# One load of V in two transfers, in every third batch: a grouped-query attention backward kernel on one core

## The chip, the cores and the metric

The kernel runs on one core of one Trainium2 chip. The metric is the device time of one execution in microseconds (us); the time of before is the median of three runs. The core has a matrix engine (PE), a vector engine (DVE), a scalar engine (ACT), a general engine (POOL) and a synchronisation engine (SP). Here SP issues the loads and POOL issues the stores; sixteen DMA engines carry both.

## The reference

Grouped-query attention, forward and backward, in bf16: 32 batches, 32 query heads on 4 key/value heads, 4 queries, 2048 keys, depth 128.

```python
def _fwd_reference(q, k, v):            # q [32,32,4,128], k and v [32,4,2048,128]
    k = jnp.repeat(k, rep, axis=1)
    v = jnp.repeat(v, rep, axis=1)
    scale = D ** -0.5
    scores = jnp.einsum("bhqd,bhkd->bhqk", q, k) * scale
    p = _softmax(scores, axis=-1)
    return jnp.einsum("bhqk,bhkd->bhqd", p, v)

def reference(q, k, v, grad_out):
    ...
    _out, _vjp = jax.vjp(_f, q, k, v)
    _grads = _vjp(grad_out)
    return (_out, *_grads)              # out, dq, dk, dv
```

K, V, dK and dV are 2 MB a batch each. So each batch reads 4 MB and writes 4 MB, and everything else is small beside that.

## The kernel before

A batch is one unit of work. Its 128 query rows (8 query heads x 4 queries for each of 4 key/value heads) fill the 128 partitions, and its 2048 keys lie as 128 partitions of 16 keys. Partition p of head h holds keys 16p to 16p+15, which are 4096 bytes in a row in memory.

The steps of a batch b have names, and three strings (HEAD, STEADY, TAIL) write out by hand in which order they are issued; every engine works through its own part of that order. One pass of STEADY is one batch long and mixes steps of several batches:

- LK(b) and LV(b) issue the loads: four transfers for K and four for V, one for each head, each [128 partitions x 4096 bytes], 512 KB, on SP's queue (lines 154 and 160). Both stand in the order one batch and more ahead of their use.
- KT and VT (helper `turned`, line 181) turn K and V on PE with an identity matrix; DVE copies the result out of PSUM (line 183).
- S and EX make the scores and the exponentials (lines 198, 211, 222); NRM makes the normalisers on POOL (line 231); ET and dST turn the rows (line 248).
- O and dQ gather over the keys (line 264), from the V tile and the K tile as loaded. dP makes the score gradients (line 338).
- dV and dK (helper `outer`, line 303) are outer products, eight steps each; ACT copies each from PSUM into an output tile (line 307), and after the eighth POOL issues the tile's two stores of 1 MB (line 326).

K has three buffers, V has two, and dK and dV share four output tiles. A load can be issued when its buffer has been read for the last time, and an output tile can be refilled when its two stores have landed.

Each transfer raises a semaphore sixteen times when its parts land. SP's transfers take eight such semaphores in turn, so that a transfer also waits until the eighth transfer before it on SP has landed. With eight loads a batch, that is the load in the same place one batch earlier. POOL's transfers take eight others.

Of the kernel before, what the change touches and what calls it, by code (L numbers as in the profile page):

```python
# [81 lines left out]
def kernel(ctx: ExitStack, tc: tile.TileContext, q, k, v, grad_out, out_0, out_1, out_2, out_3):  # L82
    nc = tc.nc
    B, Hq, Sq, D = q.shape
    NH, Sk = k.shape[1], k.shape[2]
    P = 128
# [41 lines left out]
    v_v = v.rearrange("b h (p c) d -> b h p (c d)", c=C)  # L128
# [27 lines left out]
    def LV(b):  # L156
        S = st[b]
        S["v"] = v_pool.tile([P, NH, C, D], BF16, name="v_sb")
        for h in range(NH):
            nc.sync.dma_start(out=S["v"][:, h].rearrange("p c d -> p (c d)"), in_=v_v[b, h])  # L160

    def bank16():

# [170 lines left out]
    def dP(b, i):  # L334
# [6 lines left out]
        banks.give(t)  # L341

    table = {"LK": LK, "LV": LV, "QDT": QDT, "O": O, "dQ": dQ, "NRM": NRM}
    for i, c in enumerate("ab"):
        for n, f in (("S", S_), ("EX", EX), ("dP", dP), ("ET", ET), ("dST", dST)):
# [16 lines left out]
    with tc.manual_schedule():  # L362

        for w in HEAD.split():
            w, b = w.split("@")
# [5 lines left out]
        for w in TAIL.split():  # L371
            w, b = w.split("@")
# [31 lines left out]
```

## Time and profile before

| | |
|---|---|
| median of three runs | 701.2 us (699.08, 701.52, 701.2) |
| the profiled execution's own time | 698.71 us |
| its span, first to last instruction | 696.7 us |
| granted clock of PE, mean | 0.980 |
| busy: PE, DVE, ACT, POOL | 626.0, 584.5, 569.1, 302.7 us |
| bytes moved by DMA | 274.44 MB, mean 394 GB/s |
| loads on SP's queue (q1, hardware) | 37920 packets, 134.50 MB |
| transfers on POOL's queue (q0, software) | 37536 packets, 138.16 MB |
| instruction fetches (q8) | 96 packets, 1.57 MB |

A packet is what one DMA engine moves at one time: here a row of 4096 bytes in most cases. The trace keeps the start, the duration, the size and the queue of every packet, and the time of each of the sixteen landings of every transfer. It does not keep which of the sixteen engines a packet or a landing belongs to.

The profile's busy shares are averages over the span. The span has a start of some 40 us in which the first loads come in, a long stretch in which one pass of STEADY follows another, and an end of some 40 us after the last load.

### The profile page before, as it was taken

The numbers are of one execution on the slowest core, as the hardware profiler recorded it, in microseconds if no ns is written. First come the engines' busy times: TensorE is split into PE (matmuls) and PEld (weight loads), VectorE is DVE, ScalarE is ACT, GpSimd is POOL, SyncE is SP. The second block draws the span as 40 slices with busy tenths as digits, with TensorE's granted clock in tenths as the row PEclk, the third lists the DMA queues.
The fourth block names the chain that finished last, engine by engine and source line by source line (L and its number), as shares of the span: only waits on it lengthen the run. The fifth ranks groups of instructions, "written<-read, shape, count | busy, mean of one in ns | idle before, by whom it ended". The sixth has DMA issues, their size and how long they took to land.

```text
span 696.7 us, 28064 instructions
## 1 busy us (share of the span) xinstructions
PE 626.0 (90%) x12352; PEld 454.1 (65%) x12352; DVE 584.5 (84%) x992; ACT 569.1 (82%) x673; POOL 302.7 (43%) x506
## 2 busy tenths in 40 slices
PE   5899999999998989979999798998998889998982
PEld 4577776677676656666666676667766677666661
DVE  5999999999997998869988688888988869898960
ACT  0698989899887989869888687887888868888994
POOL 1355443555454435443354424544434543345452
PEclk9999999999999999999999899999999989999997
DMA  9989999999999999999999999999999999999767
GB/s 339 400 317 411 417 415 416 416 413 415 417 415 417 414 417 416 417 409 412 415 415 413 373 397 398 400 410 382 416 416 417 415 340 393 415 414 415 289 257 274
DMA packets 75577, 274.44 MB, mean 394 GB/s; under 512 B 8448, under 2 KB 8448, under 8 KB 75456
## 3 DMA queue, kind: packets, MB, share of 16 engines
q0 software_dynamic: 37536, 138.16, 49.3%
q1 hardware_dynamic: 37920, 134.50, 48.9%
q8 instruction: 96, 1.57, 0.8%
q14 instruction: 25, 0.20, 0.1%
HBM read 136.31 MB, written 136.31 MB: 391 GB/s over the span
## 4 chain that ended last, share of the span: by engine, by line
PE 43%; DMA 33%; ACT 6%; DVE 5%; POOL 5%; issue 5%; SPq 0%; POOLq 0%; DVEq 0%; ACTq 0%
PE banks L181 18%; DMA k_sb<-in_k_dram 15%; DMA out_dram<-dk 12%; PE banks L303 10%; PE banks L264 7%; ACT dv L307 5%; PE banks L248 5%; DMA out_dram<-dv 4%; PE banks L198 3%; POOL dop L231 2%; DMA v_sb<-in_v_dram 2%; DVE kt L183 2%; DVE ds L338 1%; ACT dk L307 1%; POOL qp L231 1%
## 5 line engine op out<-in xcount | busy, mean ns | idle before, releaser
L307 ACT CAST dv<-banks 128x1024 bf16<-128x1024 f32 x256 | 245.5, 1028 | 56.9 <-PE banks L303 56.3
L307 ACT CAST dk<-banks 128x1024 bf16<-128x1024 f32 x256 | 250.7, 1025 | 34.5 <-PE banks L303 23.6
L183 DVE COPY kt<-banks 128x1024 bf16<-128x1024 bf16 x256 | 164.3, 680 | 8.3 <-PE banks L181 8.3
L183 DVE COPY vt<-banks 128x1024 bf16<-128x1024 bf16 x256 | 166.2, 680 | 1.3 <-PE banks L181 0.9
L181 PE MATMUL banks<-ident,k_sb 128*128 128x128 bf16 x2048 | 145.8, 221 | 13.1 <-DMA k_sb<-in_k_dram 8.6
L181 PE MATMUL banks<-ident,v_sb 128*128 128x128 bf16 x2048 | 143.5, 220 | 14.3 <-ACT dv L307 9.7
L231 POOL TENSOR_SCALAR dop<-do_sb,rinv 32x128 bf16<-32x128 bf16 x128 | 76.7, 599 | 181.3 <-PE banks L303 118.9
L181 PEld LDWEIGHTS <-k_sb 128*128 128x128 bf16 x2048 | 120.8, 99 | 41.9 <-issue 31.7
L181 PEld LDWEIGHTS <-v_sb 128*128 128x128 bf16 x2048 | 122.2, 98 | 28.7 <-issue 23.3
L303 PE MATMUL banks<-dop,e 64*128 64x256 bf16 x1024 | 99.3, 276 | 15.1 <-POOL dop L231 11.3
L326 POOL DMA_DIRECT2D out_dram<-dv x62 | 43.7, 709 | 138.0 <-ACT dv L307 67.6
L338 DVE SCALAR_TENSOR_TENSOR ds<-banks,delta,e 128x1024 bf16<-128x1024 f32 x64 | 82.2, 1284 | 17.3 <-PE banks L198 14.3
L303 PE MATMUL banks<-qp,ds 64*128 64x256 bf16 x1024 | 86.4, 272 | 2.1 <-ACT dk L307 1.4
L231 POOL TENSOR_SCALAR qp<-q_sb,srinv 32x128 bf16<-32x128 bf16 x128 | 78.1, 610 | 10.7
L222 ACT ACTIVATE e<-banks,negb 128x1024 bf16<-128x1024 f32 x64 | 70.7, 1111 | 8.6 <-DVE negb L214 8.5
L211 DVE TENSOR_REDUCE m<-banks 128x1 f32<-128x1024 f32 x64 | 75.1, 1215 | 0.9 <-PE banks L198 0.9
L303 PEld LDWEIGHTS <-e 64*128 64x128 bf16 x1024 | 34.0, 94 | 63.1 <-issue 46.7
L250 DVE COPY et<-banks 128x1024 bf16<-128x1024 bf16 x64 | 41.3, 686 | 29.6 <-PE banks L248 29.6
L303 PEld LDWEIGHTS <-ds 64*128 64x128 bf16 x1024 | 42.2, 94 | 28.8 <-ACT dv L307 13.1
L326 POOL DMA_DIRECT2D out_dram<-dk x62 | 44.0, 713 | 13.6 <-DMA out_dram<-dk 13.0
L250 DVE COPY dst<-banks 128x1024 bf16<-128x1024 bf16 x64 | 43.5, 681 | 5.5 <-PE banks L248 3.6
L248 PE MATMUL banks<-ident,ds 128*128 128x128 bf16 x512 | 39.4, 221 | 7.1 <-ACT dk L307 6.8
(39 smaller groups left out, 484.1 us busy)
## 6 DMA issues: line engine op xcount, KB each, us to landing
k_sb<-in_k_dram SPq DMA_DIRECT2D x128, 512.0 KB, 13.8
v_sb<-in_v_dram SPq DMA_DIRECT2D x128, 512.0 KB, 18.6
out_dram<-dv POOLq DMA_DIRECT2D x64, 1024.0 KB, 23.6
out_dram<-dk POOLq DMA_DIRECT2D x64, 1024.0 KB, 22.1
out_dram<-o_sb POOLq DMA_DIRECT2D x32, 32.0 KB, 23.2
out_dram<-dq_sb POOLq DMA_DIRECT2D x32, 32.0 KB, 16.2
q_sb<-in_q_dram POOLq DMA_DIRECT2D x7, 128.0 KB, 21.9
do_sb<-in_grad_out_dram POOLq DMA_DIRECT2D x7, 128.0 KB, 22.0
```

The costliest lines, as they stand in the source:

```text
L181: nc.tensor.transpose(out=ps[:, 4 * hh + j, :], in_=S[which][:, 2 * (i % 2) + hh, 4 * (i // 2) + j, :], identity=ident[:])
L183: nc.vector.tensor_copy(out=S[f"{which}t{i}"][:], in_=ps)
L211: nc.vector.reduce_max(out=S["m"][:, i:i + 1], in_=S[f"s{i}"][1], axis=AX.X)
L222: nc.scalar.activation(out=S[f"e{i}"][:], in_=ps, func=ACT.Exp, bias=S["negb"][:], scale=scale, accum_out=S["l"][:, i:i + 1],)
L231: nc.gpsimd.tensor_scalar(out=t[r, h % 2, :], in0=src[r, :], scalar1=by[r, :], scalar2=None, op0=ALU.mult)
L248: nc.tensor.transpose(out=ps[:, u, :], in_=S[f"{src}{i}"][:, P * u:P * u + P], identity=ident[:])
L250: nc.vector.tensor_copy(out=S[f"{name}{i}"][:], in_=ps)
L264: nc.tensor.matmul(ps[G * h:G * h + G, :], lhsT=S[f"{xt}{c // 8}"][:, c % 8, G * h:G * h + G], rhs=S[kv][:, h, c, :], start=(c == 0), stop ...
L303: nc.tensor.matmul(ps[:, a, :, c, :], lhsT=S[f"{x}{i // 4}"][r, u:u + P], rhs=S[y][r, :, :], start=True, stop=True, tile_position=(2 * G * ...
L307: copy(out=S[name][:, :, 2 * i:2 * i + 2, :].rearrange("p h c d -> p h (c d)"), in_=banks.ap(t).rearrange("p a (j w) -> p (a j) w", j=2),)
L326: store.dma_start(out=dst[b][:, 2 * a:2 * a + 2, :], in_=o[:, 2 * a:2 * a + 2].rearrange("p h c d -> p h (c d)"))
L338: nc.vector.scalar_tensor_tensor(out=S[f"ds{i}"][:], in0=ps, scalar=S["delta"][:], in1=S[f"e{i}"][:], op0=ALU.subtract, op1=ALU.mult,)
```

## The change

In LV, the load of the fourth head (h = 3) is issued as two transfers, one of partitions 0 to 118 (119 rows) and one of partitions 119 to 127 (9 rows), in every third batch from batch 3 on: batches 3, 6, 9 and so on to 30, ten in all. All other loads stay as they are, and so do the bytes and the order of the steps.

```diff
@@ -157,7 +157,9 @@
         S = st[b]
         S["v"] = v_pool.tile([P, NH, C, D], BF16, name="v_sb")
         for h in range(NH):
-            nc.sync.dma_start(out=S["v"][:, h].rearrange("p c d -> p (c d)"), in_=v_v[b, h])
+
+            for r in (slice(0, 119), slice(119, P)) if h == NH - 1 and b % 3 == 0 and b else (slice(0, P),):
+                nc.sync.dma_start(out=S["v"][r, h].rearrange("p c d -> p (c d)"), in_=v_v[b, h, r])
```

## The prediction

> **What bounds the kernel now.** I read the page's slices first, then the windows by stage, the chain of waits, SP's own waits, and last the trace's records of packets and landings.
>
> ```profile
> span 696.7 us, 28064 instructions
> PE 626.0 (90%) x12352; PEld 454.1 (65%) x12352; DVE 584.5 (84%) x992; ACT 569.1 (82%) x673; POOL 302.7 (43%) x506
> DMA  9989999999999999999999999999999999999767
> GB/s 339 400 317 411 417 415 416 416 413 415 417 415 417 414 417 416 417 409 412 415 415 413 373 397 398 400 410 382 416 416 417 415 340 393 415 414 415 289 257 274
> ```
>
> No compute engine is full, but the DMA row is full until the last tenth, at 415 to 417 GB/s in slice after slice. The windows by stage (us, busy times, clock, DMA share, GB/s) say the same:
>
> ```profile
> 40.00:120.00 80.00, 78.11 (x1620) 57.17 (x1607) 74.03 (x128) 72.37 (x87) 37.79 (x62) 1.00 1.00 397
> 120.00:240.00 120.00, 113.67 (x2262) 82.35 (x2264) 108.67 (x184) 105.00 (x125) 57.23 (x94) 1.00 1.03 415
> 400.00:560.00 160.00, 147.75 (x2846) 106.37 (x2843) 138.50 (x234) 134.35 (x159) 68.91 (x113) 0.98 1.02 406
> ```
>
> PE is nearly full to 120 us and has gaps from there on. The chain of waits between 195 and 262 us shows what fills them: three times a wait of 17 us for a K load, with 4 us of PE work between.
>
> ```profile
> 199.11 16.95 DMA k_sb<-in_k_dram
> ...
> 220.24 16.81 DMA k_sb<-in_k_dram
> ...
> 241.24 17.01 DMA k_sb<-in_k_dram
> ```
>
> Pass follows pass every 21.1 us there, and 19.5 us between 53.3 and 72.8 us, where PE's L181 leads the chain. So compute needs 19.5 us a batch, and DMA sets 21.1.
>
> Next, is it all sixteen DMA engines, or some? The landing records answer. For the fourth V load of a batch (us from the start; 1st, 7th, 8th, 15th, 16th landing):
>
> | batch | 1st | 7th | 8th | 15th | 16th |
> |---|---|---|---|---|---|
> | 7 | 140.8 | 143.1 | 143.7 | 144.9 | 147.2 |
> | 13 | 264.1 | 265.4 | 267.7 | 268.8 | 274.3 |
> | 17 | 343.7 | 345.1 | 351.6 | 353.2 | 358.6 |
> | 27 | 556.4 | 558.3 | 558.7 | 562.7 | 570.4 |
>
> A load is whole only at its 16th landing. By batch 17 the sixteen have parted into seven early ones, eight later ones, and one alone. That one engine comes last by 5 to 9 us. From batch 7 to 13 the 7th landing moves on by 20.4 us a batch, the 8th and 15th by 20.65, the 16th by 21.18; the 16th holds 21.2 to batch 27. So **one slow DMA engine paces the kernel**, and the other fifteen have slack of 0.5 to 0.8 us a batch. Its packets are long: between 674.05 and 675.20 us it alone still has stores, with packets of 160 to 176 ns (mean 169), where 159 ns is the usual row and the next starts 4 ns before the end (a pitch of 155).
>
> **The change, part by part.** Removed: ten loads of 128 rows. Before, 32768 packets of 4096 bytes make 256 loads, so each load is 16 equal shares of 8 rows. Added: ten of 119 and ten of 9 rows.
>
> *The shares.* No row shows a transfer of 119 rows. The bounds are: shares as even as can be (15 engines with 8 rows or fewer; nothing changes), or equal shares as all 256 loads have them. 119 is 7 x 17, so equal shares on at most sixteen engines mean seven engines with 17 rows; nine rows are nine engines with one. I take the equal shares, because every load of before has them. Then seven engines carry 17 or 18 rows instead of 8, and at least seven of the others carry none. By the Trainium skill ("DMA: Bandwidth & Descriptors", the section on why a DMA increments its semaphore by 16) the engine count is the largest divisor up to 16 and the lowest-numbered engines are taken; that would be 7 and 9, and this split.
>
> *What it costs the seven.* Ten more rows x 155 ns = 1.55 us a changed batch, 0.52 us a batch on average. *What it saves the others:* 7 or 8 rows; on the slow engine at 165 ns (between 159 and 169, both queues mixed) 1.16 to 1.32 us, 0.39 to 0.44 a batch.
>
> *The sum, if the seven are the early seven.* The slow engine goes from 21.18 to 20.76, the seven from 20.4 to 20.9 (from packets alone, 128 x 0.155 + 0.4 for small ones = 20.25, to 20.8). The new pace is 20.8 to 20.9, still above compute's 19.5. The DMA-paced stretch runs from batch 3's V (whole at 58.7 us) to batch 31's (655.8 us): 28 batches x 0.28 to 0.38 = 8 to 10.6 us. I take 9.5. On the profiled 698.7 us that is 689.2; that execution lay 2.5 us under the median of 701.2, so I state 691.5 as the median.
>
> *Issue and waits on SP.* Ten more issues of 0.33 us (the row of L160) are 3.3 us on a queue that is idle for most of a batch: nothing. But the eight semaphores shift by one. SP already waits there:
>
> ```profile
> SPq L154 <- PE banks L303: 293.5, 29, 13.4
> SPq L160 <- PE banks L303: 80.2, 27, 5.1
> SPq L160 <- DMA v_sb<-in_v_dram: 72.3, 46, 2.5
> ```
>
> The nine rows wait for the first K load of the same batch, which lands 1.9 to 2.8 us after the fourth V load's issue from batch 7 to 27. Each V load of the next batch waits for its right-hand neighbour, 2.5 us later. Queued behind on SP are only later loads. What covers it is the slow engine's backlog: loads take 21 us from issue to landing, so 2.6 us off that queue starve nobody. Without cover it is 10 x 2.6 = 26 us.
>
> *Nine rows as a transfer of their own.* Back-to-back loads at the start land 1.27 us apart (6.36, 7.63, 8.96), which is 8 x 0.155 plus a semaphore packet of 9 ns; I see no fixed price. The same page's rules for kernel authors advise against two transfers to disjoint partitions, and its fixed part is about 2.0 us each: by that, 10 x 2.0 = 20 us slower if none of it overlapped. The start of this trace disagrees with such a price between queued transfers.
>
> *Landing of the split load.* On the seven, ten rows interleaved with stores are up to 3.1 us. The 15th landing leads the 16th by 5 to 9 us from batch 13 on, so it stays hidden; at batches 3, 6 and 9 the lead is 0.7 to 3.1 us, but SP's semaphore isn't yet the limit there. Nothing added.
>
> **The rivals.**
> *B, slower: the slow engine is one of the seven.* It then gets ten more rows x 0.165 = 1.65 us, ten times: 16.5 us on an engine with no slack, 717.7. It decides as soon as the slow one is among the seven. For it: counted blindly, 7 in 16. Against: the groups of 7, 8 and 1 look like halves of eight, one half with the odd one in it; I put an odd one at an end of a half, and seven counted from one end of the sixteen then take it in one place of four. That is my choice, no row shows it. By the same skill page ("Latency and other measured facts") engines 7 and 15 are usually the slow ones, which the lowest seven would spare; this trace has one slow engine, not two.
> *C, nothing: the slow one is spared, but the seven lie in the later eight.* These go from 20.65 to 21.17, as slow as the slow engine was: 701, within 4 us. For it: the eight are more than the seven. What sets them back are the 96 instruction fetches of 16 KB (the one followed at 427 us cost 1.15 us with the row behind it): 110 us over eight engines and 32 batches is 0.43 us a batch, about their distance.
> *N: 119 rows are spread nearly evenly.* 701. Against: the equal shares so far.
> *L: the waits on SP's shifted semaphores show.* 5 to 26 us slower, 706 to 727. For it: V comes just in time (weight loads wait for it 21 times, 0.7 us at the longest). Against: the backlog.
>
> **How the numbers follow.** My forecast, A, has 0.44; C 0.27; B 0.19; L 0.06; N 0.04. A measurement of this kernel can tell about 0.5% (3.5 us) from no change. A is faster but for 0.01; C splits 0.05 faster, 0.12 same, 0.10 slower, since seven engines near the bound seldom wait less than one. So faster 0.43 + 0.05 = 0.48; same 0.12 + 0.04 = 0.16; slower 0.01 + 0.10 + 0.19 + 0.06 = 0.36. A alone lies in 687 to 697. The range runs from 686 (a relief of 1.32 us fully kept is 13 us, and two more) to 712, which takes in C, N and the lower part of L; it leaves out B, the rest of L and A's edge, 0.2 or a little more.
>
> **What would show it.** In the landings of a 119-row load, nine of sixteen would come at once, seven late. The 16th landing of the fourth V load should move on by about 20.85 us a batch, and the lone engine's distance should shrink. The waits of 17 us for K should shorten. Landings parted further, with passes near 21.7 us, would mean B; an unchanged pace with a smaller lone distance C; no early landings N; longer SP waits at L160 with idle DMA slices L.

## The result and the profile after

The changed kernel takes 721.1 us (median; 720.52 to 721.87) beside 700.77 us for the kernel before on the same chip: a ratio of 1.0298, 95% interval 1.0277 to 1.0319. It is slower by 20 us. The forecast A (691.5 us, faster) is wrong, and so is the range to 712 us; the rival B stood at 717.7 us.

The page of the changed kernel (its profiled span, then the DMA row in 40 slices, GB/s in the same slices, and the shares of the chain of waits):

```profile
span 718.9 us, 28084 instructions
...
DMA  9989999999999999999999999999999999999667
GB/s 334 384 323 412 416 415 416 398 415 414 384 389 395 415 393 362 412 393 393 369 391 391 379 400 402 372 379 409 400 410 389 396 380 358 383 416 412 259 238 277
...
DMA 48%; PE 38%; DVE 4%; ACT 4%; issue 4%; POOL 1%; SPq 0%; POOLq 0%; ACTq 0%; DVEq 0%
```

The bytes are the same and the DMA row still shows nines, but from the eighth slice on the rate falls below 400 GB/s again and again, where it lay at 409 to 417 from slice 4 to slice 22 before. The nines hide it: they are means over sixteen engines, in tenths. Of the chain, DMA holds 48%. In the kernel before it held 33%:

```profile
PE 43%; DMA 33%; ACT 6%; DVE 5%; POOL 5%; issue 5%; SPq 0%; POOLq 0%; DVEq 0%; ACTq 0%
```

The windows by stage have the same loss, in 120 to 240 us for instance (us, busy PE, PEld, DVE, ACT, POOL, clock, DMA share, GB/s), 401 GB/s for 415:

```profile
120.00:240.00 120.00, 107.58 (x2177) 77.72 (x2164) 100.66 (x172) 97.94 (x116) 55.73 (x92) 0.99 1.02 401
400.00:560.00 160.00, 142.46 (x2844) 104.67 (x2848) 134.55 (x229) 128.56 (x154) 64.60 (x107) 0.99 1.01 393
```

The chain of waits from 228 to 300 us shows where the time goes. Batch 12 is a split one, its fourth V load is issued at 242.29 us, and the K load behind it is the second line:

```profile
230.69 16.64 DMA k_sb<-in_k_dram
...
251.54 20.83 DMA k_sb<-in_k_dram
...
276.55 17.01 DMA k_sb<-in_k_dram
```

The wait for K behind a split V load is 20.8 us, the others are 17 us as before: about 4 us in one pass. The landing records say which part of the transfer is late (us from the start, landings in order). The first record of each line comes 0.4 to 0.5 us after the issue, ahead of all queued loads, and I read it as carrying no data. The prediction expected nine early landings of the 119 rows in its place; the trace has this one.

```
batch 12, 119 rows, issued 242.29: 242.7 | 252.1 252.5 256.1 256.7 257.6 257.9 | 266.9
batch 12,   9 rows, issued 245.01: 245.5 | 248.8 249.5 252.5 252.9 256.5 257.2 258.0 258.3 | 267.4
batch 21, 119 rows, issued 441.73: 442.2 | 450.2 450.3 451.0 451.0 451.4 452.7 | 464.6
```

119 rows land in seven shares and 9 rows in nine, as the equal shares had it. But one of the seven, and one of the nine, lands 9 to 12 us after all others: the lone engine is in both. Over the ten split loads this distance of the 119 rows grows from 0.3 us in batch 3 and 3.2 us in batch 6 to 11 to 14 us from batch 15 on. On that engine the load before, of 8 rows, lands at 261.49, the 17 rows at 266.90 and the one row at 267.36. So 18 rows take 5.9 us where the 8 rows before took 2.7 (from 258.75).

### The profile page after: what moved, and what is told of

The parts are those of the page before. It is cut to its first block, busy times and chain, and to the rows that moved or that the text cites. A ratio compares the mean times of both kernels' runs of the same rounds, so it can differ in the third digit from the quotient of the medians.

```text
span 718.9 us, 28084 instructions
## 1 busy us (share of the span) xinstructions
PE 629.3 (88%) x12352; PEld 458.2 (64%) x12352; DVE 588.0 (82%) x992; ACT 568.9 (79%) x673; POOL 301.7 (42%) x506
## 4 chain that ended last, share of the span: by engine, by line
DMA 48%; PE 38%; DVE 4%; ACT 4%; issue 4%; POOL 1%; SPq 0%; POOLq 0%; ACTq 0%; DVEq 0%
DMA k_sb<-in_k_dram 48%; PE banks L183 17%; PE banks L305 10%; PE banks L266 6%; PE banks L250 3%; ACT dv L309 3%; PE banks L200 2%; DVE kt L185 1%; DVE m L213 1%; DVE ds L340 1%; ACT dk L309 1%; DVE vt L185 1%; POOL dop L233 0%; PE banks L173 0%; POOL out_dram L321 0%
## 5 line engine op out<-in xcount | busy, mean ns | idle before, releaser
L185 DVE COPY kt<-banks 128x1024 bf16<-128x1024 bf16 x256 | 166.3, 683 | 22.2 <-PE banks L183 21.9
L183 PE MATMUL banks<-ident,k_sb 128*128 128x128 bf16 x2048 | 151.9, 225 | 31.0 <-DMA k_sb<-in_k_dram 26.6
L183 PE MATMUL banks<-ident,v_sb 128*128 128x128 bf16 x2048 | 145.9, 221 | 24.3 <-ACT dv L309 10.7
L183 PEld LDWEIGHTS <-k_sb 128*128 128x128 bf16 x2048 | 124.0, 101 | 62.0 <-issue 31.2
L183 PEld LDWEIGHTS <-v_sb 128*128 128x128 bf16 x2048 | 123.7, 99 | 39.2 <-issue 21.8
L305 PE MATMUL banks<-dop,e 64*128 64x256 bf16 x1024 | 97.2, 273 | 10.8 <-issue 6.0
L233 POOL TENSOR_SCALAR qp<-q_sb,srinv 32x128 bf16<-32x128 bf16 x128 | 77.3, 604 | 10.7
L200 PE MATMUL banks<-vt,qdt 128*32 128x512 bf16 x512 | 40.6, 385 | 3.1 <-ACT dv L309 1.5
```

Of the source, the lines that this page charges most:

```text
L183: nc.tensor.transpose(out=ps[:, 4 * hh + j, :], in_=S[which][:, 2 * (i % 2) + hh, 4 * (i // 2) + j, :], identity=ident[:])
L185: nc.vector.tensor_copy(out=S[f"{which}t{i}"][:], in_=ps)
L200: nc.tensor.matmul(ps[G * h:G * h + G, a, :], lhsT=S["qdt"][:, col, G * h:G * h + G], rhs=xt[:, 4 * (h % 2):4 * (h % 2) + 4, :].rearrange( ...
L233: nc.gpsimd.tensor_scalar(out=t[r, h % 2, :], in0=src[r, :], scalar1=by[r, :], scalar2=None, op0=ALU.mult)
L305: nc.tensor.matmul(ps[:, a, :, c, :], lhsT=S[f"{x}{i // 4}"][r, u:u + P], rhs=S[y][r, :, :], start=True, stop=True, tile_position=(2 * G * ...
```

## The experiments

All are the changed kernel with another rule for which rows of V make one transfer. Only the tuple in the loop header differs, so the diffs show that line. Unless said otherwise they change V's fourth head in batches 3, 6, ... 30.

**Which engine is the slow one.** Single parts of r and 16 - r rows, with r from 1 to 8, are probes: r equal shares of one row take the first r engines, if every transfer takes them in the same order.

```diff
- (slice(0, 119), slice(119, P)) if h == NH - 1 and b % 3 == 0 and b else ...
+ (slice(0, 112), slice(112, 105 + b // 2 + 4), slice(105 + b // 2 + 4, P)) if h == NH - 1 and b % 2 == 0 and 8 <= b <= 22 else ...
```

> Batches 8, 10, ... 22 load V's fourth head as 112 + r + (16 - r) rows, with r = 1, 2, ... 8. Theory S (one slow DMA engine, and it is one of the seven that took the 119 rows): the part of r rows has r landings, one row each, and from some r on, between 1 and 7, its last landing comes late by the lone engine's distance (4 to 9 us after the others); all parts of 16 - r rows (9 to 15 landings) have that late landing too. Theory T (the late landing of the 119 rows belonged to the transfer, as its last share, and not to an engine): the parts of r rows have no late landing at any r from 1 to 8. Time under S: within 4 us of before, since each engine gets 7, 8 or 9 rows.

The one run of it took 698.43 us. Landings with data of the parts of r rows:

```
r=3  244.8 245.2 246.1
r=4  284.7 284.7 286.1 286.5              (112 rows of the same load: 282.5 ... 290.5, 297.2)
r=5  327.0 327.3 327.4 327.7 | 340.1      (112 rows: 326.6 ... 333.2, 339.6)
r=6  368.4 368.5 368.9 369.2 372.4 | 383.1
r=8  455.5 455.5 455.6 455.6 455.7 457.2 457.4 | 469.5
```

Up to four shares none is late. From five on exactly one is, by 10.7 to 12.4 us, and the parts of 15 to 8 rows have a last landing apart from the others every time. That is theory S, and it names the engine: the fifth in the order in which transfers take them. The first four belong to the early ones (at r = 5 they land from 327.0 to 327.7 us, beside the earliest seven of the 112 rows from 326.6 to 327.6).

**Two transfers, even shares.** 112 + 16 rows.

> The same ten loads as 112 + 16 rows: two transfers as in the change, but seven rows and one row for each of sixteen engines, eight as before. Theory S (the seven extra shares on the slow engine make the time): no difference, 699 to 703 us. Rival L (the shifted semaphores on SP, or a price of a transfer of its own): it keeps what L is worth, 5 to 20 us slower; 706 to 721 us.

699.37 us, ratio 0.9993 (0.9974 to 1.0013). Splitting a load in two, with its issue on SP and the shifted semaphores, costs nothing that can be seen. SP's wait at the V loads, which was to show L, did grow, from 72.3 us before to 114.0 us in this run (first line) and 192.6 us in the change (second line):

```profile
SPq L162 <- DMA v_sb<-in_v_dram: 114.0, 68, 2.6
SPq L162 <- DMA v_sb<-in_v_dram: 192.6, 91, 6.0
```

But the growth to 114.0 us costs no time, and the DMA slices of the change are not idle, as L would have had them. L is out for the change.

**120 + 8 rows.**

> The same ten loads as 120 + 8 rows. With equal shares that is fifteen engines with eight rows, eight engines with one more, and one engine with none or one. Theory S (the slow engine is among the seven lowest): it carries nine rows instead of eight, one row more ten times, at the 0.2 us that a row cost in the change 2 us: 701 to 704 us. A rival S' (a slow engine at the far end, which the 119-row transfer left out, and another cause for the loss): the far engine is relieved of eight rows, ten times 1.3 us, about 690 us.

Ratio 1.0003 (0.9987 to 1.0020), 700.77 us: 0.2 us, at most 1.4. The relief of a far engine is not there (S' said 690 us). One extra row a load was expected to cost 2 us and cost less than that; at this size I can't tell it from nothing.

**Half as many.** 119 + 9 rows in every sixth batch.

> 119 + 9 rows in every sixth batch only (batches 6, 12, 18, 24, 30): five loads instead of ten. Theory S with a price for each split load: half of the 20.4 us, about 711 us (709 to 713). Rival M (the backlog hides single ones, and only a rate of one in three exceeds the slack): less than a quarter, below 706 us.

Ratio 1.0146 (1.0119 to 1.0173), 710.5 us: 10.2 us, half of the change's. Each 119 + 9 load has its price of about 2 us, and single ones aren't hidden.

**More and fewer rows on the slow engine.** 125 + 3 rows (five engines with 25) and 110 + 18 rows (ten and two).

> The same ten loads as 125 + 3 rows: five engines with 25 rows, three with one. The slow engine, the fifth, gets 25 rows instead of 8: 17 more, where the change gave it 10 more. Theory S with a price for each row of 0.204 us (20.4 us for 100 rows): 34.7 us slower, 735 us. With the predicted 0.165 us: 28 us slower, 728 us. A price for each split load whatever its share: 720 us.

> The same ten loads as 110 + 18 rows: eleven engines with ten rows, nine of them with two more. The slow engine gets 12 rows instead of 8, 4 more. Theory S with 0.204 us a row: 8.2 us slower, 708 us; with 0.165 us 6.6 us, 707 us. A threshold (the backlog hides a small share): within 2 us of before.

125 + 3: ratio 1.0464 (1.0443 to 1.0484), 732.8 us, 32.5 us slower. 110 + 18: ratio 1.0096 (1.0079 to 1.0112), 706.9 us, 6.7 us slower. Set against the extra rows that the fifth engine carries in ten loads:

| split | extra rows x 10 loads | slower, us | us a row |
|---|---|---|---|
| 112 + 16 | 0 | -0.5 | |
| 120 + 8 | 10 | 0.2 | 0.02 |
| 110 + 18 | 40 | 6.7 | 0.17 |
| 119 + 9 | 100 | 20.9 | 0.21 |
| 125 + 3 | 170 | 32.5 | 0.19 |

(The us are the ratio times 701.) From four rows on, the time goes with the slow engine's rows at 0.17 to 0.21 us each. There is no price for a split load as such. In these splits other engines get longer shares too, but they are not the late ones: from batch 6 on the last share of the 125 rows lands 3.4 to 13.6 us after the other four, and the last of the 110 rows 2.5 to 13.7 us after the other ten.

**The same split on V's first head.**

```diff
- ... if h == NH - 1 and b % 3 == 0 and b else ...
+ ... if h == 0 and b % 3 == 0 and b else ...
```

> The change's ten splits, 119 + 9 rows, on V's first head instead of its fourth. Theory S (ten more rows of work on the slow engine, wherever they stand): the same 20 us, 718 to 723 us. Rival K (the loss comes from the K load that stands right behind the fourth head, and three V loads between them would take it up): under 710 us.

Ratio 1.0326 (1.0304 to 1.0347), 723.7 us, just above the expected 723. The three V loads between it and the next K take nothing up: in batch 12 the last landing trails the one before it by 5.5 us at the split part, and by 5.8 us still at the first K load behind the three. K (the rival) is out.

**The slow engine spared, others loaded.** 68 + 60 rows (the first four engines 21 rows, the fifth 4) and 124 + 4 rows (the first four 32, all others none).

> The same ten loads as 68 + 60 rows. By equal shares that is four engines with 17 rows and fifteen with 4: the first four carry 21 rows (13 more), the fifth, which the run with r rows showed to be the slow one, carries 4 instead of 8. Theory S (only the slow engine counts): it is relieved of 4 rows ten times, at 0.165 to 0.2 us a row 6.6 to 8 us; the first four are among the early seven and get 13 x 0.155 = 2.0 us a split load, 0.67 us a batch, from 20.3 to 20.9, still below 21.2. Faster: 692 to 696 us beside 700. Rival T (any engine with a long share makes the load late and the kernel slower): 13 more rows instead of 10, 20 us or more slower, 720 us and up.

> The same ten loads as 124 + 4 rows: the first four engines carry 32 rows (24 more), all others none (8 fewer), the slow one too. Theory S: the slow engine gains 8 rows x 0.165 to 0.2 us x 10 = 13 to 16 us, but the four early engines get 24 x 0.155 = 3.7 us a split load, 1.24 us a batch, from 20.3 to 21.5, which is above 21.2: they take over, 5 to 10 us slower, 705 to 710 us. Rival T (any long share costs as in the change, 2.04 us for ten rows): 24 rows cost 4.9 us each, 49 us slower, 749 us.

68 + 60: ratio 1.0054 (1.0034 to 1.0073), 703.8 us. 124 + 4: ratio 1.0354 (1.0330 to 1.0378), 724.4 us. Neither theory was right. T would have had 720 and 749 us, so a long share on an early engine costs far less than on the slow one. But S promised a gain from 68 + 60, and there is a loss of 3.8 us; and 124 + 4 lost 25 us instead of 5 to 10. The landings name the miss: in batch 24 of 68 + 60 the four shares of 17 rows land at 506.9, 510.3, 512.3 and 514.7 us, while ten of the fifteen shares of 4 rows are there by 501.3. The four with long shares have become the last. My reading, which no run isolates, is this: I had counted their extra work over three batches (2.0 us) against their slack, but the delay comes at once, and with a store row between two load rows it is 13 x 0.31 = 4 us or 24 x 0.31 = 7.4 us. In the run of 68 + 60 rows the last landing of a batch's first K load trails the 15th by 3.9 us at most, so little lead is left to hide it.

**Relief in small steps.** 112 + 4 + 4 + 4 + 4 rows in every batch but the first, and the same with V's second head in odd batches too.

```diff
- (slice(0, 119), slice(119, P)) if h == NH - 1 and b % 3 == 0 and b else ...
+ (slice(0, 112), slice(112, 116), slice(116, 120), slice(120, 124), slice(124, P)) if h == NH - 1 and b else ...
```

> V's fourth head in every batch but the first as 112 + 4 + 4 + 4 + 4 rows: seven rows for all sixteen engines and four times one row for each of the first four. The slow engine gets 7 rows instead of 8 in every batch, the first four 11. Theory S: 31 rows less on the slow engine at 0.165 to 0.2 us, 5 to 6 us faster, 694 to 696 us; the first four go from 20.3 to 20.75 us a batch and stay under it, and three more rows delay their share by 0.9 us only. Rival L (twelve transfers a batch through eight semaphores let SP wait for landings that come too late): slower than before, 705 us or more.

> The same, and V's second head likewise in every odd batch: 1.5 rows a batch less on the slow engine, 4.5 more on the first four. Theory S: 47 rows at 0.165 to 0.2 us, 7 to 9 us faster, with the first four at 20.3 + 0.7 = 21.0 us a batch, so that they just become the bound: 692 to 697 us. Rival L: slower than the kernel with one such head a batch, by as much again as that one lost.

The first: ratio 0.9989 (0.9973 to 1.0005), 699.7 us, no gain; neither range has it, S's 694 to 696 us or L's 705 us and more. The second: ratio 1.0172 (1.0149 to 1.0196), 713.3 us, slower, and by more than L said, as the first lost nothing. Two causes offer themselves, and no run separates them. One is L: SP's own waits in the first (line, waited for: us in total, times, longest) are led by landings, and by those of the other tile:

```profile
SPq L154 <- DMA v_sb<-in_v_dram: 216.3, 108, 3.1
SPq L162 <- DMA k_sb<-in_k_dram: 174.1, 96, 3.2
```

In the changed kernel these two rows are small:

```profile
SPq L162 <- DMA k_sb<-in_k_dram: 19.5, 9, 2.4
SPq L154 <- DMA v_sb<-in_v_dram: 12.0, 8, 2.6
```

With twelve transfers a batch and eight semaphores, a K load waits for a V load of the batch before, and a small part of V for a K load of its own batch. The other cause is the longer shares of the first four engines. In the first version, in 23 of the 24 batches from 8 to 31, the small part's last landing comes 0.2 to 0.6 us after the last landing of the 112 rows, and the small parts lie on the first four engines alone; in the second it is so in every batch from 5 on. So one of the first four, and no longer the fifth, is the last to finish the head: the fifth is relieved, but the pace has passed to others.

**Relief seldom and late.** 68 + 60 rows in batches 12, 18, 24 and 30.

```diff
- (slice(0, 119), slice(119, P)) if h == NH - 1 and b % 3 == 0 and b else ...
+ (slice(0, 68), slice(68, P)) if h == NH - 1 and b in (12, 18, 24, 30) else ...
```

> 68 + 60 rows in batches 12, 18, 24 and 30 only, where the lone engine's lead over the others is 4 us and more. The slow engine carries 16 rows less in all. If the loss with ten such loads came from the first four engines, which 13 extra rows at 0.31 us (a store row between two load rows) hold up by 4 us at a time when they need six batches to make it up: now 2.6 to 3.2 us faster, 697 to 698 us. If a relief of the slow engine brings nothing because the other engines follow close behind: the same as before within 1 us.

Ratio 0.9973 (0.9956 to 0.9990), 698.7 beside 700.95 us. It is the one version whose interval lies wholly below the kernel before, by 1.9 us (0.7 to 3.1). That is between the two expectations, and the interval reaches into both. Here the first four engines stay ahead of the fifth: in batch 18 their four shares have landed by 372.9 us, and the last of the 60 rows lands at 381.5 us.

## Why the prediction was wrong

- **What bounds the kernel: right, as far as added rows show it.** One slow DMA engine sets the pace, and in the splits that load it the time follows its rows. What a relief of it is worth stays open: the most that one brought is 1.9 us, and with more of it the first four engines became the last.
- **The shares: right.** 119 rows went to seven engines and 9 rows to nine. The Trainium skill's rule on the count and on the lowest engines ("DMA: Bandwidth & Descriptors", on why a DMA increments its semaphore by 16) agrees with the probes. Each probe of r rows had r landings with data, and the late one appears from r = 5 on and stays.
- **The step that failed: which engines the seven are.** The prediction put the slow engine at an end of a half of the sixteen and wrote "That is my choice, no row shows it". It is the fifth, and so among the seven. Counted blindly the chance was 7 in 16; the choice lowered it to 0.19 and left B out of the range. The remark of the Trainium skill ("DMA: Bandwidth & Descriptors", "Latency and other measured facts") that engines 7 and 15 are usually the slow ones led the same wrong way, as the lowest seven would have spared both. Here the measurement says the fifth, and one only.
- **B's price: a term too small.** "ten more rows x 0.165 = 1.65 us" measured 2.1 us (20.9 us in ten loads). The 0.165 us is a row's own time, taken between 159 and 169 ns. In the loads' queue 18 rows took 5.9 us, which is 0.33 us a row, two row times, as if a store row went between every two load rows. The pass after a split was longer by 3 us: the 16th landing of the first K load moves on by 23.9 to 24.7 us there (batches 10, 13, ... 28) and by 20.2 to 21.2 in the passes between. Over the batches 6 to 30 it moves on by 22.0 us on average, beside 21.2 before; longer passes were the prediction's own sign for B. So a part of the 3 us is made up later. That the rest is lost because the slow engine's stores run short meanwhile is argued, not shown; it fits that they trail less: in batch 23 the 16th landing of dV's second store comes 7.0 us after the 15th, before 17.1 us.
- **Issue, waits on SP, the extra transfer: right for this change** (112 + 16 rows: no difference). The 2.0 us that the Trainium skill ("DMA: Bandwidth & Descriptors", "Anatomy of one DMA") gives as a transfer's fixed part, measured there on transfers that GpSimd issues, do not show either on SP's loads. By that figure twenty transfers in place of ten would have cost an estimated 20 us.
- **"Landing of the split load": not safe on early engines either.** The prediction took the lead of the lone engine as cover for ten late rows. 68 + 60 rows show that 13 more rows on early engines already make them the last; ten on them alone were not tried.
- **N and C.** The shares refute N. C falls with the same step: it needs the slow engine spared, and the slow engine is among the seven. That instruction fetches set eight engines back, which C gave as a reason, no run tests.

## What to carry to other kernels

Before rows of a transfer are shifted between DMA engines, find out which engine paces the kernel and whether the new shares take it: a single run with probes of 1 to 8 rows, and the landings of each, decides that. Where a tuned kernel hangs on one engine, a row that is added there costs about its own time or somewhat more (here 0.17 to 0.21 us from four rows a load on; one row a load cost nothing that could be seen), and here it held up the loads behind it by two row times at first. Rows taken off that engine must go somewhere, and the engines that get them can become the last. If no row of the profile tells which of two engines is meant, the range has to hold both.

## What the runs showed of the hardware

- A load from SP's queue whose rows aren't a multiple of sixteen goes to fewer engines: 119 rows to seven, 125 to five, 124 to four, 68 to four, by their landings with data. They are counted from the same end in all splits tried, as the late landing is in every transfer of five shares and more of the probe run and in none of one to four.
- One DMA engine of this core, the fifth in that order, is slower than the other fifteen where loads and stores run together: 21.2 us a batch beside 20.4 to 20.65 from batch 7 to 13, and the probes of five to eight rows all find it there. Before the first store lands, at 33.8 us, no engine falls back: over nine loads in a row, from 19.6 to 29.9 us, the 16th landing stays 0.8 us behind the 15th. Why the fifth is slow, no run shows.
- The fifth is the slow one on a second chip as well. By the record the probes ran on chip 11; on chip 4 the five shares of 125 rows have one late landing from batch 6 on, and the four shares of 68 rows in batches 12, 18, 24 and 30 have none.
- A mean DMA share of 1.00 doesn't say that sixteen engines are busy in the same way: in the changed kernel the share is 1.00 or more in every window from 40 to 656 us, and yet the rate from 120 to 560 us is lower by 3 to 5%.
